# Scores as block-diagonal products and six product tiles in the head, in place of scores as 64-row tiles and four product tiles

## The chip, the cores and the metric

The kernel runs on one core of a Trainium2 chip. The metric is device time in microseconds, the median of three runs. The kernel before takes 285.92 us (285.66 to 286.01).

## The reference

Linear attention without a softmax, a root-mean-square norm for each head, then a two-layer network with an ELU between the layers, over 8 batches of 576 rows, 8 heads of 64:

```python
kv = np.einsum('bhsd,bhse->bhde', k, v)
out = np.einsum('bhsd,bhde->bhse', q, kv)
rms = np.sqrt(np.mean(out * out, axis=-1, keepdims=True) + 1e-06)
out = out / rms * g_norm
x = out.transpose(0, 2, 1, 3).reshape(B * S, H * D)      # 4608 x 512
h = x @ w_in                                             # 512 x 2048
g = np.where(h > 0.0, h, np.exp(np.minimum(h, 0.0)) - 1.0)
return g @ w_out                                         # 2048 x 512
```

Inputs and output are float32; the products run in bfloat16 with float32 sums.

## The kernel before, in words

The 4608 rows are cut into nine groups of 512. Group T from 0 to 7 holds the first 512 rows of batch T; group 8 holds the last 64 rows of all eight batches. Each group has an attention part and a network part. The network part is 128 TensorE products of 128x128 weights on 512 columns: 64 for the first layer (`mm1(T, i)`, i = 0 to 7, eight products each, two tiles of 512 columns of float32 in PSUM) and 64 for the second (`mm2(T, j, f0, f1)`, j = 0 to 3 blocks of 128 rows, sums over sixteen f; `mm2_quarter` does four f).

All instructions stand in an order written out by hand (`manual_schedule`). While group T runs its first layer and group T-1 its second, the attention of group T+1 is put between them: `kv` (72 tiles of 64x64), scores `se_mm`, squares, sums, `inv_rms` (Ln and Exp), `scale_rows`, then the turn to x transposed, by TensorE (`x_t`, groups 1 and 2) or by a DMA transpose (`x_dma`: pieces `xd`, then `xg` multiplies by g). `elu` follows each `mm1`: Exp on ScalarE, then on VectorE min(e, 1) - 1 and a max with h straight from PSUM; where `relu` is set, ScalarE also writes Relu(h) to SBUF (`elu_h`) and VectorE adds.

PSUM after the head: one `at` tile of two banks for attention, two `ps_m1` tiles of two banks, two `ps_m2` tiles of one bank. A tile's next user waits until the last has been read.

The scores (L202 to L220): for each of four row blocks j and four head pairs p, two 64-row products, one for each head l of the pair, on 64 columns of `kv_sb`, the two into different banks, so that two run beside each other. From group 3 on both halves of the scores are made after `mm1` step 3 (L760 to L762): half 0 in the `at` tile, half 1 in the two `ps_m2` tiles, from where ScalarE copies them to SBUF (`se_sb`, L283). `scale_rows` (L238) takes two VectorE steps for each half.

The head, group 0 (L482 to L671): all of it waits for loads. POOL issues them in order, k and v of batch 0 in eight pieces, w_in in four slices of 512 columns (L498), q of batch 1, then k and v of batch 1 around the first slice of w_out (L502 to L506); a ninth POOL load is issued only when the first has landed, and so on. Meanwhile TensorE turns q, makes kv and the scores of four column blocks c, transposed; squares go to ScalarE (`square_first`, A) but for the last, which VectorE makes in two steps (V: L585, L586); `mean_first` sums over a head by a product with a matrix of means; `log_first`, `exp_first` on ScalarE; `scale_first` on VectorE writes x0[c]. `idle` puts products with zeros between, into a bank that nobody reads. L663 to L671 then start the first layer with four product tiles (f = 0 to 3), c by c, and steps 2 to 7 follow, the turn of q of batch 1 in between (L680). L689 to L720 hold kv, scores and turns of batch 1 between the quarters of group 0's second layer; the w_out slices 1 to 3 are issued at L678 and L684.

Of the kernel before, what the change touches and what calls it, by code (L numbers as in the profile page):

```python
# [16 lines left out]
def kernel(  # L17
# [44 lines left out]
    kv_sb = const.tile([P, B, NPAIR, D], BF16, name="kv_sb")  # L62
# [72 lines left out]
    def load_w_in(s):  # L135
        cols = slice(s * 512, s * 512 + 512)
        nc.gpsimd.dma_start(  # L137
            out=w_in_sb[:, :, cols], in_=moe_w_in.rearrange("(c p) f -> p c f", p=P)[:, :, cols]
        )
# [13 lines left out]
    def q_tile(b):  # L153
        bf["q", b] = qkvp.tile([P, J, H, D], BF16, name="q_bf", tag="q")
        st = raw.pop(("q", b))
        if b < B:
            return st.rearrange("p (h j d) -> p j h d", h=H, j=J)
        return st.rearrange("p (j h d) -> p j h d", h=H, j=J)
# [26 lines left out]
    def q_t_single(q_pk, qt_ps, p):  # L185
        for j in range(J):
            for l in range(2):
                nc.tensor.transpose(
                    qt_ps[l * 64 : l * 64 + 64, p, j * P : j * P + P],
# [4 lines left out]
    def q_t_mm(q_sb, qt_ps, p):  # L194
        for j in range(J):
            nc.tensor.transpose(
                qt_ps[:, p, j * P : j * P + P],
                q_sb[:, j, 2 * p : 2 * p + 2, :],
                ident,
            )  # L200

    def se_mm(T, h, qT, banks):  # L202

        for jj in range(2):
            j = 2 * h + jj
            for p in range(NPAIR):
                s, u = p // 2, p % 2
                for t in range(1 if T < B else 2):
                    rows = slice(0, P) if T < B else slice(t * 64, t * 64 + 64)
                    for l in range(2):  # L210
                        ls = slice(l * 64, l * 64 + 64)
                        nc.tensor.matmul(  # L212
                            banks[l].rearrange("p (j u s e) -> p j u s e", j=2, u=2, s=2)[
                                rows, jj, u, s, :
                            ],
                            lhsT=qT(p, j)[ls, rows],
                            rhs=kv_sb[ls, T if T < B else 2 * j + t, p, :],
                            start=True,
                            stop=True,
                        )  # L220
# [17 lines left out]
    def scale_rows(xs, se, ss):  # L238
        for l in range(2):
            nc.vector.tensor_tensor(  # L240
                out=xs.rearrange("p j (u l s e) -> p l j u s e", u=2, l=2, s=2)[:, l].rearrange(
                    "p j u s e -> p (j u) s e"
                ),
                in0=se[:, l, :].rearrange("p (a s e) -> p a s e", s=2, e=D),
                in1=ss[:, 8 * l : 8 * l + 8]
                .rearrange("p (a s) -> p a s", s=2)
                .to_broadcast([P, 4, 2, D]),
                op=ALU.mult,
            )

    def attention(T):
        st = {}

        def q_t():
# [3 lines left out]
            for p in range(NPAIR):  # L258
                q_t_single(raw["q", T], qt_ps, p)
# [12 lines left out]
        def se(homes):  # L272

            for h, home in homes.items():
                if home is None:
                    home = at_tile(FP32).rearrange("p (l f) -> p l f", l=2)
                pair = isinstance(home, list)
                banks = home if pair else [home[:, l, :] for l in range(2)]
                se_mm(T, h, st["qT"], banks)
                if pair:  # L280
                    home = attp.tile([P, 2, G], FP32, name="se_sb", tag="se_sb", bufs=1)
                    for l in range(2):
                        nc.scalar.copy(home[:, l, :], banks[l])  # L283
                st["se", h] = home

        def norm(h):

            def squares():
                st["sq", h] = square(st["se", h], 2)
# [7 lines left out]
            def scale():  # L297
# [3 lines left out]
                scale_rows(rows, st.pop(("se", h)), st.pop(("ss", h)))  # L301

            return squares, sums, inv, scale
# [58 lines left out]
        def kv_out(us):  # L362
            nc.scalar.copy(
                kv_sb[:, T].rearrange("p (s u) e -> p s u e", s=2)[:, :, us],
                st["kv"][:, :, 0:P].rearrange("p s (u e) -> p s u e", u=2)[:, :, us],
            )
# [8 lines left out]
        pieces = {"kv": kv_all, "q": q_t, "qd": q_dma, "se": se}  # L375
# [6 lines left out]
        for h in range(2):  # L382
            for name, piece in zip(("sq", "sum", "inv", "mul"), norm(h)):
                pieces[f"{name}{h}"] = piece
# [5 lines left out]
    def mm1(T, i, cols=(slice(0, 512),), relu=False, spare=False, between=()):  # L390
# [4 lines left out]
        if spare:  # L395
            h_ps = [ps_m2.tile([P, G], FP32, name="h_ps", tag="mm2") for _ in range(2)]
            parts = [(a, a + 1, h_ps[a].rearrange("p (a t) -> p a t", a=1)) for a in range(2)]
        else:
            both = ps_m1.tile([P, 2, G], FP32, name="h_ps", tag="mm1")
# [91 lines left out]

    packed_kv(0)
# [5 lines left out]
    for s in range(4):  # L498
        load_w_in(s)
    fetch_packed_q(1)  # L500
    packed_kv(1)
    for name in "kv":  # L502
        fetch_packed_kv(name, 1, slice(0, 2))
    load_w_out(0)
    for name in "kv":
        fetch_packed_kv(name, 1, slice(2, 4))  # L506
# [9 lines left out]
    fetch_q(0)  # L516
# [17 lines left out]

# [331 lines left out]
```

## Time and profile before

| what | us |
|---|---|
| median of three runs | 285.92 |
| the profiled execution, its own time | 285.66 |
| its span, first to last instruction | 283.9 |
| TensorE busy | 274.1 |
| VectorE busy | 161.2 |
| ScalarE busy | 152.8 |
| POOL busy | 53.1 |
| from the first product of the first layer to the end of the span | 268.6 |

All times in the profile are counted from the start of the span; the profiled execution's own time holds 1.8 us more, around the span. The granted TensorE clock was 1.000. A timeline line has a start, a duration, engine and line, what is written and read, shapes and count, and in brackets the idle time before it with what ended it. A matmul's duration includes its way through the array, so the distance from one start to the next is what it costs on TensorE: 512 columns have a duration of 379 ns and a distance of 216 ns. Some matmul records are missing; the distance then still tells.

### The profile page before, as it was taken

What the parts mean: (1) busy time and instruction counts of PE and PEld (TensorE: products, weight loads), DVE (VectorE), ACT (ScalarE), POOL (GpSimd) and SP (SyncE); (2) the same over time, 40 slices, a digit from 0 to 9 for tenths busy, and PEclk for the clock granted to TensorE, in tenths of its full rate; (3) what the DMA queues carried; (4) which work ended last, traced back from release to release, by engine and by line L of the source; (5) the groups of instructions that cost most, each with busy time, mean ns of one, the idle gap of its engine ahead of it and who ended that gap; (6) DMA issues with size and microseconds to landing.
All of it is one profiled execution on the core that took longest, in us unless ns stands there. A gap on an engine that the chain in (4) does not pass through costs nothing.

```text
span 283.9 us, 5147 instructions
## 1 busy us (share of the span) xinstructions
PE 274.1 (97%) x2115; PEld 129.6 (46%) x2145; DVE 161.2 (57%) x235; ACT 152.8 (54%) x217; POOL 53.1 (19%) x93
## 2 busy tenths in 40 slices
PE   7899999999999999999999999999999999999994
PEld 2444454445444444444444444444444444444444
DVE  2458561779378646934694458544864486444400
ACT  2779544766496337633773378246923692333311
POOL 7834302341431241004210421002000000000000
PEclk9999999999999999999999999999999999999999
DMA  7999999797993596356953794355233123010122
GB/s 193 204 207 202 206 203 178 224 167 135 177 173 57 150 158 158 74 144 82 194 122 113 111 195 104 101 132 157 39 92 94 77 39 99 10 76 0 75 74 74
DMA packets 55963, 35.98 MB, mean 127 GB/s; under 512 B 32772, under 2 KB 53508, under 8 KB 55940
## 3 DMA queue, kind: packets, MB, share of 16 engines
q0 software_dynamic: 20192, 17.30, 39.7%
q1 hardware_dynamic: 35348, 17.83, 23.2%
q10 hardware_dynamic: 400, 0.52, 0.6%
q8 instruction: 16, 0.26, 0.4%
q14 instruction: 7, 0.06, 0.1%
HBM read 36.70 MB, written 9.44 MB: 163 GB/s over the span
## 4 chain that ended last, share of the span: by engine, by line
PE 80%; DMA 11%; DVE 4%; issue 1%; ACT 1%; POOL 1%; DVEq 0%; POOLq 0%
PE h_ps L406 36%; PE o_ps L453 36%; PE o_ps L825 5%; DMA w_in_sb<-in_moe_w_in_dram 5%; DMA w_out_sb<-in_moe_w_out_dram 5%; DMA k_pk<-in_k_dram 2%; PE at L177 1%; DVE gT L437 1%; DVE xs L240 1%; DVE ss L229 1%; POOL w_in_sb L137 1%; PE at L212 1%; PE se_ps L212 1%; DVE elu_e L429 0%; PE at L316 0%
## 5 line engine op out<-in xcount | busy, mean ns | idle before, releaser
L406 PE MATMUL h_ps<-xT,w_in_sb 128*128 128x512 bf16 x556 | 130.7, 379 | 0.3
L453 PE MATMUL o_ps<-w_out_sb,gT 128*128 128x512 bf16 x489 | 117.9, 379 | 1.8 <-DMA w_out_sb<-in_moe_w_out_dram 0.5
L418 ACT ACTIVATE elu_e<-h_ps 128x1024 bf16<-128x1024 f32 (+1 forms) x75 | 73.1, 982 | 82.6 <-PE h_ps L406 81.0
L406 PEld LDWEIGHTS <-w_in_sb 128*128 128x128 bf16 x560 | 53.2, 98 | 64.5 <-DVE xT L344 1.7
L453 PEld LDWEIGHTS <-gT 128*128 128x128 bf16 x512 | 49.8, 98 | 59.5 <-issue 0.3
L429 DVE TENSOR_SCALAR elu_e<-elu_e 128x1024 bf16<-128x1024 bf16 (+1 forms) x76 | 32.3, 425 | 75.4 <-ACT elu_e L418 75.4
L437 DVE TENSOR_TENSOR gT<-elu_e,h_ps 128x1024 bf16<-128x1024 bf16 (+1 forms) x56 | 64.1, 1145 | 5.8
L466 ACT COPY o_sb<-o_ps 128x512 f32<-128x512 f32 x32 | 18.5, 586 | 17.4 <-PE o_ps L453 17.4
L229 DVE TENSOR_REDUCE ss<-sq 128x16 f32<-128x1024 bf16 x16 | 19.3, 1217 | 7.7 <-ACT sq L224 6.9
L151 POOL COPY q_bf<-q_pk 128x512 bf16<-128x512 bf16 x24 | 14.9, 648 | 26.3 <-DMA q_pk<-in_q_dram 22.6
L424 ACT ACTIVATE elu_h<-h_ps 128x1024 bf16<-128x1024 f32 x19 | 19.3, 1015 | 0.0
L437 DVE TENSOR_TENSOR gT<-elu_e,elu_h 128x1024 bf16<-128x1024 bf16 x19 | 13.5, 713 | 3.6 <-ACT elu_h L424 2.4
L825 PE MATMUL o_ps<-w_out_sb,gT 128*128 128x512 bf16 (+1 forms) x79 | 14.0, 336 | 0.1
L125 POOL COPY gate<-qT 1x1 bf16<-1x1 bf16 x6 | 1.1, 179 | 61.5 <-DMA qT<-q_bf 61.5
L240 DVE TENSOR_TENSOR xs<-at,ss 128x512 bf16<-128x512 f32 x18 | 11.5, 681 | 1.2 <-ACT ss L236 1.2
L104 POOL DMA_DIRECT2D q_pk<-in_q_dram x14 | 10.6, 764 | 3.6 <-issue 1.9
L825 PEld LDWEIGHTS <-gT 128*128 128x128 bf16 x80 | 7.7, 98 | 6.4 <-DVE gT L437 0.4
L224 ACT ACTIVATE sq<-at 128x1024 bf16<-128x1024 f32 x9 | 9.4, 1044 | 1.5 <-PE at L212 1.5
L118 POOL DMA_DIRECT2D k_pk<-in_k_dram x12 | 8.4, 700 | 5.4 <-DMA w_in_sb<-in_moe_w_in_dram 2.5
L118 POOL DMA_DIRECT2D v_pk<-in_v_dram x12 | 8.5, 708 | 2.2 <-DMA w_in_sb<-in_moe_w_in_dram 1.8
L833 ACT COPY o_last<-o_ps 128x512 f32<-128x512 f32 (+1 forms) x5 | 2.5, 500 | 10.8 <-PE o_ps L825 10.8
L177 PEld LDWEIGHTS <-k_pk 64*64 64x64 bf16 x576 | 6.5, 107 | 3.8 <-issue 3.6
(71 smaller groups left out, 123.0 us busy)
## 6 DMA issues: line engine op xcount, KB each, us to landing
out_dram<-o_sb SPq DMA_DIRECT2D x16, 512.0 KB, 3.0
q_pk<-in_q_dram POOLq DMA_DIRECT2D x14, 256.0 KB, 5.3
k_pk<-in_k_dram POOLq DMA_DIRECT2D x6, 576.0 KB, 8.4
v_pk<-in_v_dram POOLq DMA_DIRECT2D x6, 576.0 KB, 11.5
w_in_sb<-in_moe_w_in_dram POOLq DMA_DIRECT2D x4, 512.0 KB, 10.6
w_out_sb<-in_moe_w_out_dram POOLq DMA_DIRECT2D x4, 512.0 KB, 15.3
st_q<-in_q_dram SPq DMA_DIRECT2D x2, 512.0 KB, 4.8
st_q<-in_q_dram SPq DMA_DIRECT2D x16, 64.0 KB, 2.5
```

The lines of the kernel that those rows point to most:

```text
L118: nc.gpsimd.dma_start(out=raw[name, b].rearrange("p h j d -> p h (j d)")[:, hs], in_=in_[:, hs])
L151: eng.tensor_copy(out=out_, in_=in_)
L229: nc.vector.reduce_sum(out=ss, in_=sq.rearrange("p c (h e) -> p (c h) e", h=H), axis=AX.X)
L240: nc.vector.tensor_tensor(out=xs.rearrange("p j (u l s e) -> p l j u s e", u=2, l=2, s=2)[:, l].rearrange("p j u s e -> p (j u) s e"), in0 ...
L406: nc.tensor.matmul(h_ps[a][:, cs], lhsT=w_in_sb[:, c, f * P : f * P + P], rhs=x(c, cs), start=(c == 0), stop=(c == KC - 1),)
L418: nc.scalar.activation(e[:, lo:hi, :], ps, AF.Exp)
L424: nc.scalar.activation(h[:, lo:hi, :], ps, AF.Relu)
L429: nc.vector.tensor_scalar(out=e[:, lo:hi, :], in0=e[:, lo:hi, :], scalar1=1.0, scalar2=1.0, op0=ALU.min, op1=ALU.subtract,)
L437: nc.vector.tensor_tensor(out=gT[T][:, 2 * i + lo : 2 * i + hi, :], in0=e[:, lo:hi, :], in1=h, op=ALU.add if relu else ALU.max,)
L453: nc.tensor.matmul(o_ps[T, j], lhsT=gT[T][:, f, j * P : j * P + P], rhs=w_out_sb[:, f, :], start=(f == 0), stop=(f == FC - 1),)
L466: nc.scalar.copy(o_sb[T][:, j % 2, :], o_ps.pop((T, j)))
L825: nc.tensor.matmul(ps, lhsT=gT[B][:, f, j * P : j * P + P], rhs=w_out_sb[:, f, cols], start=(f == 0), stop=(f == FC - 1),)
```

## The change

Scores: `bd_kv` replaces `kv_sb`. It holds for each pair of heads a 128x128 matrix with the two heads' kv on the diagonal and zeros beside them (a memset once). One product of 128 rows on 128 columns replaces the two 64-row tiles; in the last group two products with 64 weight columns replace four tiles. `kv_out` writes the two diagonal blocks in two ScalarE copies. `scale_rows` becomes one VectorE step. From group 3 on, half 0 of the scores is made after `mm1` step 1 and half 1 after step 3, both in the `at` tile, with sums and scale one step later each, and no product takes the Relu path; the second layer's pieces stand at steps 0 to 6. In group 1 half 0 of the scores of batch 2 moves into the first layer (after step 6), and its two turns stand together.

Head: the six products of steps 0 to 2 start in the head's own banks, w_in comes in five slices, the w_out slices 0 and 1 are issued ahead of k and v of batch 1, the fourth square goes to ScalarE, blocks 0 to 2 take other places among the idle products, and the mean of block 3 follows the first four products. q of batch 0 is cast into a tile in the order of the head pairs. Steps 3 to 7 follow; then the second layer's quarter 0, the turn of q of batch 1, three pieces of quarter 1, kv of batch 1, the last piece, and its scores.

```diff
-    kv_sb = const.tile([P, B, NPAIR, D], BF16, name="kv_sb")
+    bd_kv = const.tile([P, B, NPAIR, P], BF16, name="bd_kv")
...
-    def se_mm(T, h, qT, banks):
-
-        for jj in range(2):
-            j = 2 * h + jj
-            for p in range(NPAIR):
-                s, u = p // 2, p % 2
-                for t in range(1 if T < B else 2):
-                    rows = slice(0, P) if T < B else slice(t * 64, t * 64 + 64)
-                    for l in range(2):
-                        ls = slice(l * 64, l * 64 + 64)
-                        nc.tensor.matmul(
-                            banks[l].rearrange("p (j u s e) -> p j u s e", j=2, u=2, s=2)[
-                                rows, jj, u, s, :
-                            ],
-                            lhsT=qT(p, j)[ls, rows],
-                            rhs=kv_sb[ls, T if T < B else 2 * j + t, p, :],
-                            start=True,
-                            stop=True,
-                        )
+    def se_mm(T, j, qT, se_ps):
+
+        ov = se_ps.rearrange("p (u l s e) -> p u l s e", u=2, l=2, s=2)
+        for p in range(NPAIR):
+            s, u = p // 2, p % 2
+            if T < B:
+                nc.tensor.matmul(
+                    ov[:, u, :, s, :],
+                    lhsT=qT(p, j),
+                    rhs=bd_kv[:, T, p, :],
+                    start=True,
+                    stop=True,
+                )
+            else:
+                for l in range(2):
+                    nc.tensor.matmul(
+                        ov[l * 64 : l * 64 + 64, u, :, s, :],
+                        lhsT=qT(p, j)[:, l * 64 : l * 64 + 64],
+                        rhs=bd_kv[:, 2 * j + l, p, :],
+                        start=True,
+                        stop=True,
+                    )
...
+    def scale_rows(xs, se_ps, ss, n):
+        nc.vector.tensor_tensor(
+            out=xs.rearrange("p c (h e) -> p (c h) e", h=H),
+            in0=se_ps.rearrange("p c (h e) -> p (c h) e", h=H),
+            in1=ss.to_broadcast([P, n * H, D]),
+            op=ALU.mult,
+        )
...
+        def se(h):
+
+
+            def product(se_ps=None):
+                if se_ps is None:
+                    se_ps = at_tile(FP32).rearrange("p (c f) -> p c f", c=2)
+                for c in range(2):
+                    se_mm(T, 2 * h + c, st["qT"], se_ps[:, c, :])
+                st["se", h] = se_ps
+                st["sq", h] = square(se_ps, 2)
...
+            bd_v = bd_kv[:, T].rearrange("p (s u) e -> p s u e", s=2)
+            for l in range(2):
+                ls = slice(l * 64, l * 64 + 64)
+                nc.scalar.copy(
+                    bd_v[ls, :, us, ls],
+                    st["kv"][ls, :, 0:P].rearrange("p s (u e) -> p s u e", u=2)[:, :, us],
+                )
...
+    edges = (0, 512, 768, 1280, 1664, 2048)
+    for lo, hi in zip(edges, edges[1:]):
+        load_w_in(slice(lo, hi))
+    load_w_out(0)
     fetch_packed_q(1)
+    load_w_out(1)
     packed_kv(1)
-    for name in "kv":
-        fetch_packed_kv(name, 1, slice(0, 2))
-    load_w_out(0)
-    for name in "kv":
-        fetch_packed_kv(name, 1, slice(2, 4))
+    for hs in (slice(0, 2), slice(2, 4)):
+        for name in "kv":
+            fetch_packed_kv(name, 1, hs)
...
+    nc.vector.memset(bd_kv, 0.0)
...
-    def square_first(c, eng):
-        if eng is A:
-            nc.scalar.activation(sq0[c], se0[c], AF.Square)
-        else:
-            nc.vector.tensor_copy(out=r0[c], in_=se0[c])
-            nc.vector.tensor_tensor(out=sq0[c], in0=r0[c], in1=se0[c], op=ALU.mult)
+    def square_first(c):
+        nc.scalar.activation(sq0[c], se0[c], AF.Square)
...
+    def first(fs, cs):
+        for c in cs:
+            for f in fs:
+                nc.tensor.matmul(
+                    products[f],
+                    lhsT=w_in_sb[:, c, f * P : f * P + P],
+                    rhs=x0[:, c, :],
+                    start=(c == 0),
+                    stop=(c == KC - 1),
+                )
+
+    qt_ps = turned(7)
+    turn_first(qt_ps, (2,))
+    nc.scalar.copy(qT0[:, 2, :], qt_ps[:, 0, :])
     kv_first(0)
+    idle(idle_ps, 1)
+    se0[0] = bank(6)
+    se_first(0)
+    square_first(0)
+    qt_ps = turned(0)
+    turn_first(qt_ps, (3,))
+    nc.vector.tensor_copy(out=qT0[:, 3, :], in_=qt_ps[:, 0, :])
+    idle_ps = bank(3)
+    kv_first(1)
+    mean0[0] = bank(2)
+    mean_first(0)
+    log_first(0)
+    se0[1] = bank(7)
+    se_first(1)
+    square_first(1)
+    exp_first(0)
+    g_ps = bank(1)
     nc.tensor.matmul(
         g_ps[:, 0:1],
         lhsT=g_row.rearrange("p l d -> p (l d)"),
...
         stop=True,
     )
     nc.vector.tensor_copy(out=g_col, in_=g_ps[:, 0:1])
     kv_first(2)
+    idle(idle_ps, 2)
+    se0[2] = bank(1)
+    se_first(2)
+    square_first(2)
+    mean0[1] = bank(0)
     mean_first(1)
     log_first(1)
     exp_first(1)
+    idle(idle_ps, 1)
     kv_first(3)
+    scale_first(0)
     idle(idle_ps, 1)
+    mean0[2] = bank(2)
     mean_first(2)
     log_first(2)
+    se0[3] = bank(3)
+    se_first(3)
+    square_first(3)
     exp_first(2)
+    idle(bank(0), 6)
     scale_first(1)
     scale_first(2)
+    pair = ps_head.tile([P, 2, G], FP32, name="h_ps", tag="kv")
+    products = {0: pair[:, 0, :], 1: pair[:, 1, :], 2: bank(6), 3: bank(7), 4: bank(0)}
+    first((0, 1, 2, 3), (0,))
+    mean0[3] = bank(2)
     mean_first(3)
     log_first(3)
     exp_first(3)
     scale_first(3)
+    first((0, 1, 2, 3), (1,))
+    first((4,), (0, 1))
+    first((0, 1, 2, 3, 4), (2,))
+    products[5] = bank(1)
+    first((5,), (0, 1, 2))
+    first((0, 1, 2, 3, 4, 5), (3,))
+    gT[0] = mlpg.tile([P, FC, G], BF16, name="gT", tag="gT")
+    single = [
+        [(a, a + 1, products[2 * i + a].rearrange("p (a t) -> p a t", a=1)) for a in range(2)]
+        for i in (1, 2)
+    ]
+    for i, parts in enumerate([[(0, 2, pair)]] + single):
+        elu(0, i, parts, i == 1)()
...
+    for i in range(3, 8):
+        mm1(0, i, relu=i in (3, 5, 7), home={5: "m2", 6: "at"}.get(i, "m1"))()
+    for l in range(2):
+        ls = slice(l * 64, l * 64 + 64)
+        nc.gpsimd.tensor_copy(
+            out=bd_kv[ls, 0].rearrange("p (s u) e -> p u s e", s=2)[:, :, :, ls], in_=kv0[ls]
+        )
+    for s in (2, 3):
+        load_w_out(s)
     fetch_packed_q(2)
     packed_kv(2)
     for name in "kv":
         fetch_packed_kv(name, 2)
     both = ps_m1.tile([P, 2, G], FP32, name="o_ps", tag="mm1")
     for a in range(2):
         o_ps[0, 2 + a] = both[:, a, :]
     order = (2, 3, 0, 1)
     for j in order:
         mm2_quarter(0, j, 0)
+    at["q"]()
+    for j in order[:3]:
+        mm2_quarter(0, j, 1)
+    at["kv0"]()
     at["kv1"]()
+    mm2_quarter(0, order[3], 1)
+    at["se0"]()
+    at["se1"](ps_m1.tile([P, 2, G], FP32, name="se_ps", tag="mm1"))
     for n in range(2):
         at[f"sum{n}"]()
         at[f"inv{n}"]()
     at["mul0"]()
     at["mul1"]()
     for j in order:
         mm2_quarter(0, j, 2)
     unpack_q(2, Q)
     ahead["qd"]()
     for j in order:
         mm2(0, j, 12, FC, hold=j in (2, 3))
+        if j == 2:
+            at["x0"]()
+        if j == 0:
+            at["x1"]()
...
+    def group(T, at, start, second, relu=()):
+
+
+        early, late = {}, {}
+        for name, i in start.items():
+            if name in ("se0", "se1"):
+                early.setdefault(i + 1, []).extend(("sum" + name[2], "inv" + name[2]))
+                late.setdefault(i + 1, []).insert(0, "mul" + name[2])
+            late.setdefault(i, []).append(name)
+        for i in range(9 if 8 in early else 8):
+            if i == 8:
+                for name in early[8] + late[8]:
+                    at[name]()
+                break
+            rest = mm1(
+                T, i, (slice(0, 512),), i in relu, between=[at[name] for name in early.get(i, ())]
+            )
             for piece in second.get(i, ()):
+                mm2(*piece)
+            names = late.get(i, [])
+            if i in relu and names[:1] in (["mul0"], ["mul1"]):
+                at[names.pop(0)]()
             rest()
+            for name in names:
+                at[name]()
...
+        if i == 6:
+            at["se0"]()
...
+        second = {i: [(T - 1, i // 2, 8 * (i % 2), 8 * (i % 2) + 8)] for i in range(8)}
+        if T > 2:
+            mm2(*second[0][0])
+            second = {i - 1: second[i] for i in range(1, 8)}
+        else:
+            quarters = [(1, 2 + i // 4, 4 * (i % 4), 4 * (i % 4) + 4) for i in range(2, 8)]
+            second = {i + 1: [piece] for i, piece in enumerate(quarters)}
+        at, start = ahead, {}
+        if T + 1 < NT:
+            start = {"kv": 0, "se0": 1, "xd0": 2, "se1": 3, "xd1": 4, "xg0": 5, "xg1": 6}
         if T + 2 < NT:
             at["landed"]()
             fetch(T + 2)
             ahead = attention(T + 2)
+        group(T, at, start, second, (1, 2, 4) if T == 2 else ())
```

## The prediction

> **What bounds the kernel now.** I read the busy shares and the chain of waits first, then TensorE's time by group, then its order of instructions in the groups and in the head.
>
> ```profile
> PE 274.1 (97%) x2115; PEld 129.6 (46%) x2145; DVE 161.2 (57%) x235; ACT 152.8 (54%) x217; POOL 53.1 (19%) x93
> PE 80%; DMA 11%; DVE 4%; issue 1%; ACT 1%; POOL 1%; DVEq 0%; POOLq 0%
> ```
> TensorE is busy nearly always, but busy is not the same as useful. So I cut the span where each group's first product starts.
>
> ```profile
> 0.00:15.34 15.34, 11.88 (x120) 5.51 (x122) 6.36 (x19) 8.35 (x13) 11.62 (x23) 1.00 0.99 200
> 15.34:47.69 32.35, 31.17 (x277) 15.51 (x280) 18.73 (x30) 20.64 (x31) 9.12 (x14) 1.00 1.27 205
> 47.69:72.67 24.98, 24.77 (x224) 11.99 (x224) 17.92 (x27) 15.87 (x24) 6.97 (x14) 1.00 0.85 179
> 72.67:93.63 20.96, 20.56 (x190) 9.62 (x193) 14.83 (x21) 13.79 (x19) 5.92 (x9) 1.00 0.74 118
> 93.63:122.76 29.13, 28.97 (x231) 13.56 (x233) 18.35 (x26) 16.54 (x23) 5.59 (x10) 1.00 0.67 127
> 210.17:238.56 28.39, 28.23 (x190) 12.95 (x192) 17.48 (x24) 15.73 (x22) 0.00 (x0) 1.00 0.28 75
> 238.56:266.21 27.65, 27.54 (x127) 12.43 (x128) 13.15 (x16) 10.09 (x12) 0.00 (x0) 1.00 0.10 40
> ```
> The columns are the stretch, its length, then busy time and count of PE, PEld, DVE, ACT, POOL. The last row is the last group's, with no attention beside it: 128 products of 512 columns in 27.65, 0.216 us each, without a gap. Groups 3 to 6 take 29.13 (29.14): the same 128, and 1.48 for the next group's attention. There is no other idle time there, so what an edit puts on TensorE or takes off it in these groups is the change of the time.
>
> ```profile
> 69.90 0.61 PE L316 MATMUL at<-ident,xs 128*128 128x128 bf16 x8
> 70.35 1.03 PE L453 MATMUL o_ps<-w_out_sb,gT 128*128 128x512 bf16 x4
> 106.53 1.89 PE L406 MATMUL h_ps<-xT,w_in_sb 128*128 128x512 bf16 x8
> 108.35 0.41 PE L212 MATMUL at<-kv_sb,qT 64*128 64x64 bf16 x16
> 108.59 0.40 PE L212 MATMUL se_ps<-kv_sb,qT 64*128 64x64 bf16 x16
> 108.92 1.90 PE L406 MATMUL h_ps<-xT,w_in_sb 128*128 128x512 bf16 x8
> 25.80 1.08 PE L188 MATMUL at<-ident,q_pk 128*64 128x128 bf16 x32
> 26.81 0.39 PE L406 MATMUL h_ps<-xT,w_in_sb 128*128 128x512 bf16 x1
> 36.44 5.34 PE L453 MATMUL o_ps<-w_out_sb,gT 128*128 128x512 bf16 x23 [0.37 <-DMA w_out_sb<-in_moe_w_out_dram]
> ```
> First column start, second duration; the distance of starts is what an instruction costs.
>
> **Scores, groups 3 to 6.** Removed: 32 tiles of 64 rows. The 8 products from 106.53 would let the next start at 108.26; it starts at 108.92, so the scores cost 0.66, 0.09 of it a gap ahead of the first. Added: 16 products of 128x128 over 128 columns (block-diagonal bd_kv). This product is not in the trace; the nearest row is the turn L316, the same shape in and out: 8 in 0.45 and no gap ahead or behind, 0.90 for 16. Bounds for one: 32 ns, the pitch of the half-wide L188 (32 in 1.01), would give 0.51; 82 ns (4 turns and a change of tile shape, 7.47 to 7.80) 1.31. I take 0.90, as the shape is the same: +0.24 four times, **+0.96** (-0.6 to +2.6).
>
> The Trainium skill, TensorE: Matmul & The Clock Gate, section Back-to-back issue gap, speaks against the change: pairs of weight load and product of 128 columns sustain about 81 ns. The row above shows 56 ns; by the page the four groups would lose about 2.6 in place of 0.96. I go by the row.
>
> **Scores elsewhere.** Group 7 (for the last, mixed rows): 64 tiles now, 222.27 to 224.74 less 8 products, 0.74. Then 32 products with 64 weight columns, L188's form: 1.01, and a 0.09 change of shape in each half: 1.19, **+0.45**. Groups 1 and 2: 0.89 and 2 x 0.44 now against 0.90: **+0.03**.
>
> **The head.** The chain to product 1 runs through squares, mean, Ln, Exp and scale of four column blocks. I walk it with today's durations (square 0.60, Ln 0.69, Exp 0.63, on ScalarE 0.11 less from start to start; scale 0.75; product 0.216, result after 0.38).
>
> ```profile
> 13.65 0.69 DVE L585 COPY r<-bank 128x512 f32<-128x512 f32 x1 [0.50 <-PE bank L573]
> 14.37 0.69 DVE L586 TENSOR_TENSOR sq<-r,bank 128x512 bf16<-128x512 f32 x1
> 15.12 0.39 PE L589 MATMUL bank<-sq,means 128*128 128x512 bf16 x1
> 15.34 0.38 PE L665 MATMUL at<-xT,w_in_sb 128*128 128x512 bf16 x1
> 16.93 0.75 DVE L598 SCALAR_TENSOR_TENSOR xT<-bank,g_col,r 128x512 bf16<-128x512 f32 x1 [0.54 <-ACT r L595]
> 17.93 0.59 PE L665 MATMUL h_ps<-xT,w_in_sb 128*128 128x512 bf16 x2
> ```
> Now the fourth square is two VectorE steps that end at 15.06; the mean waits for them, and the first product behind it starts at 15.34. Twelve products cover the way of block 3 from that mean to the end of its scale, 17.68.
>
> After: scores 0 at 8.6 (8.84 now), 1 at 10.1, 2 at 11.7, block 3 at 13.35; scale 0 ends 13.95, scale 1 14.85. The fourth square, on ScalarE behind Ln 1, Exp 1 and Ln 2, ends 15.1, no sooner. But the mean of block 3 stands behind four products, and six idle products end at 14.90, so product 1 starts at **14.90, -0.44** (14.7 to 15.34). Block 3's mean is then at 15.77 and its scale ends 18.35, 0.67 late; the 18 products ahead of its use end at 19.0, so that is covered by 0.65. With twelve it would cost 0.65. All 24 end at 20.30.
>
> **Group 0, rest.** Banks 4 and 5 (pair) go to product step 4, which could start at 22.03. Its holder's Exp starts 19.64, then min and max on VectorE (0.5 and 1.22 from start to start), free at 22.44: a new stall of 0.46. The first product ends at 29.39; now 30.37 with the turn of q (1.11) in it. From there: quarter 0 (3.45), turn (1.11), 12 products, so the two k/v products at 36.73; now they wait for ScalarE (0.38) and then TensorE for w_out slice 1 (0.37). These waits go, as slice 1 is loaded ahead of k and v. What is late next is k and v: the same bytes stand ahead of their second half as ahead of slice 1 now, so it lands about 36.4, used at 37.26, 0.85 of cover. Slices 2 and 3 keep their place (last landing 25.83 + 16.2 = 42.0, used at 43.17). The copies for bd_kv on POOL ahead of them (one of 0.54 now, two then) hide behind a queue that issues some 15 us before landing. Scores at 38.81, scaled by 44.1 and 45.2; the turns wait 0.09, the second's eviction (VectorE, 0.75) has 4 products (0.86) over it and costs 0.14. Group 1 starts at **47.76 against 47.69, +0.07**. Bounds: w_out slice 3 at 42.06, 16 products, two turns and 0.25 give 46.7 (-1.0); no gain in the head and these stalls twice, 48.5 (+0.8).
>
> **Covered.** memset of bd_kv: 0.27 for 256 words today, so about 1.8 for 2048, in VectorE's wait for q (1.7 to 4.75); without it 1.8 on the head. w_in in five: slice 0 lands 7.2 after its issue at 7.31, 14.5, and the next, half as wide, about 1.5 later; it is used at 16.9. Second ScalarE copy of kv (0.37), less 2 x 0.59 of score copies and 2 x 1.02 of Relu a group: off the path. In return VectorE reads two more products from PSUM (1.22 in place of 0.71) and scales in one step (as 1.22, now 1.29): 17.5 becomes about 18.4 of 29.4. Scores move to product 1: qT lands by 128.5 where POOL's gate read it; they would start near 132.3, 3.8 of cover. The last piece of the second product moves from step 7 to 6: the same 16 products. Group 1: the stall ahead of 72.67 (0.15) goes, the earlier turn waits about as long: -0.03. Group 2: its 0.26 wait near 91.7 hangs on VectorE, which saves 0.14: **-0.1**.
>
> **Sum.** 0.96 + 0.45 + 0.03 + 0.07 - 0.13 = +1.38. The profiled execution took 285.66 (span 283.9 and 1.8 around it); that gives 287.04. The median of the three, 285.92, lies 0.26 above it; I name **287.1**.
>
> **Rivals.** (A) Not slower: group 0 gets all that the loads allow. With no stall behind 14.90 it ends by landing, 46.7: -1.0 in place of +0.07, sum +0.31, 285.9 to 286.2. For it: 0.75 of waits that go. Against: the hold of the pair, from durations alone. It decides from group 1 at 47.1 or earlier, and only a further 0.6 would be faster. (B) VectorE becomes the bound in groups 3 to 7: the scores of half 1 need the at bank that half 0's scale frees, 1.1 ahead by my walk; late by 1.4, five groups lose 0.3: 288.5. For: 1.0 more PSUM reading a group. Against: group 2 runs this order in shorter steps and loses 0.26. (C) The new order of loads only moves the wait: k and v land at 38.2 rather than 36.4 and hold TensorE 0.9: 287.9. For: cover of 0.85 only. Against: equal bytes. (D) The scores run at the upper bound, 82 ns: 2.6, 0.7 and 0.9 in place of 0.96, 0.45 and 0.03: 289.8; L316 is against it.
>
> **Chances.** Forecast 0.55 (its own range 286.5 to 287.7), A 0.23, B 0.1, C 0.09, D 0.03. Within 0.2% (285.35 to 286.49, about what the measurement can tell) comes from A and the forecast's low edge: 0.2; faster, A's far end: 0.1; slower 0.7. The range leaves out D, B's far half and A's far end: 286.0 to 288.1.
>
> **What would show it.** First product at 14.9; step 4 of group 0 held by VectorE near 22; no wait for w_out slice 1, TensorE not waiting for k_pk; group 1 at 47.8; 8 scores in 0.45 with no gap; groups 3 to 6 29.36 long, group 7 28.84. I am wrong if group 1 starts before 47.1, or groups 3 to 6 stay at 29.13, or VectorE ends waits of TensorE there.

## The result, and the profile after

The changed kernel takes 287.98 us (median of six runs, 287.60 to 288.20), the kernel before 285.87 (285.66 to 287.35) beside it: a ratio of 1.0065, 95% interval 1.0043 to 1.0086. By the medians it is slower by about 2.1 us. The profiled execution took 288.11 us with a span of 285.8, against 285.66 and 283.9.

First the busy shares and the chain of waits of the changed kernel, then TensorE alone in the same stretches as before: each begins with the first product of a group of rows (the columns are the stretch, its length, busy time of PE and its instructions, then clock, DMA share and GB/s).

```profile
PE 277.1 (97%) x1976; PEld 133.8 (47%) x2006; DVE 166.6 (58%) x216; ACT 144.5 (51%) x209; POOL 54.4 (19%) x95
...
PE 93%; DMA 2%; DVE 2%; ACT 1%; issue 1%; SPq 0%; DVEq 0%
```

```profile
0.00:15.14 15.14, 12.66 (x124) 1.00 1.02 201
15.14:48.25 33.11, 31.74 (x261) 1.00 1.28 205
48.25:73.30 25.05, 24.94 (x207) 1.00 0.81 170
73.30:94.10 20.80, 20.64 (x175) 1.00 0.77 120
94.10:123.43 29.33, 29.17 (x214) 1.00 0.73 130
182.10:211.54 29.44, 29.28 (x214) 1.00 0.44 108
211.54:240.52 28.98, 28.82 (x159) 1.00 0.28 73
240.52:268.14 27.62, 27.46 (x126) 1.00 0.10 39
```

Loads have nearly left the chain of waits (11% before, 2% now), and TensorE stands in 93% of it. That looks better and is not: what TensorE has to do became longer. Set against the old stretches, the loss lies here:

| place | before | after | difference |
|---|---|---|---|
| group 1 starts (head and group 0) | 47.69 | 48.25 | +0.56 |
| group 1 | 24.98 | 25.05 | +0.07 |
| group 2 | 20.96 | 20.80 | -0.16 |
| groups 3 to 6 together | 116.54 | 117.44 | +0.90 |
| group 7 | 28.39 | 28.98 | +0.59 |
| group 8 | 27.65 | 27.62 | -0.03 |

The sum is +1.93, the whole of the span's growth. The rest of the profiled execution's +2.45 lies around the span: 1.8 us in the profiled execution of before, 1.9 to 2.3 in the six of the changed kernel. No run explains it.

The next rows are the changed kernel's order of time in the head and in group 0 (start, duration, engine, line, operation; the bracket is the idle time ahead of the row and what ended it).

```profile
13.84 1.47 PE L521 MATMUL bank<-zeros 128*128 128x512 bf16 x6
15.14 0.59 PE L599 MATMUL h_ps<-xT,w_in_sb 128*128 128x512 bf16 x2
...
21.46 1.22 DVE L422 TENSOR_TENSOR gT<-elu_e,h_ps 128x1024 bf16<-128x1024 bf16 x1
22.74 3.61 PE L391 MATMUL h_ps<-xT,w_in_sb 128*128 128x512 bf16 x16 [0.31 <-DVE gT L422]
...
36.90 0.48 PE L174 MATMUL at<-v_pk,k_pk 64*64 64x64 bf16 x36
38.02 0.48 PE L174 MATMUL at<-v_pk,k_pk 64*64 64x64 bf16 x36 [0.65 <-ACT bd_kv L345]
39.31 0.61 PE L197 MATMUL at<-bd_kv,qT 128*128 128x128 bf16 x8
39.75 0.61 PE L197 MATMUL se_ps<-bd_kv,qT 128*128 128x128 bf16 x8
40.20 4.48 PE L438 MATMUL o_ps<-w_out_sb,gT 128*128 128x512 bf16 x20
...
48.25 1.02 PE L391 MATMUL h_ps<-xT,w_in_sb 128*128 128x512 bf16 x4
```

Two waits stand out. Step 4 of the first layer starts at 22.74, just behind VectorE's maximum on the pair (21.46 and 1.22). And the second k/v product stands still 0.65 behind ScalarE's copies of the first into bd_kv. The wait for a w_out slice, which stood here before, is gone. Each run of eight score products takes 0.44 or 0.45 from start to start, and no gap follows it.

One trace stands behind each of these starts, and the start of the head varies: four kernels with this same head have their first product at 15.14, 15.16, 15.30 and 15.14 (changed, e1_tiled, e2_kvgap, e3_relu0). So a difference below 0.2 in the start of group 1 can come from the head alone; distances that begin behind it don't hold this.

### The profile page after: what moved, and what is told of

Its sections match the earlier page's. It is cut to its first block, busy times and chain, and to the rows that moved or that the text cites. A ratio compares the mean times of both kernels' runs of the same rounds, so it can differ in the third digit from the quotient of the medians.

```text
span 285.8 us, 4842 instructions
## 1 busy us (share of the span) xinstructions
PE 277.1 (97%) x1976; PEld 133.8 (47%) x2006; DVE 166.6 (58%) x216; ACT 144.5 (51%) x209; POOL 54.4 (19%) x95
## 4 chain that ended last, share of the span: by engine, by line
PE 93%; DMA 2%; DVE 2%; ACT 1%; issue 1%; SPq 0%; DVEq 0%
PE h_ps L391 41%; PE o_ps L438 37%; PE o_ps L819 5%; DMA st_q<-in_q_dram 2%; PE at L197 2%; PE at L174 2%; PE bank L599 1%; PE bank L521 1%; ACT elu_e L403 1%; PE h_ps L599 1%; PE at L391 1%; PE bank L569 1%; PE at L295 0%; DVE gT L422 0%; PE kv_ps L174 0%
## 5 line engine op out<-in xcount | busy, mean ns | idle before, releaser
L391 PE MATMUL h_ps<-xT,w_in_sb 128*128 128x512 bf16 x540 | 127.4, 379 | 0.6 <-DVE gT L422 0.3
L403 ACT ACTIVATE elu_e<-h_ps 128x1024 bf16<-128x1024 f32 (+1 forms) x72 | 70.9, 994 | 82.2 <-PE h_ps L391 80.1
L422 DVE TENSOR_TENSOR gT<-elu_e,h_ps 128x1024 bf16<-128x1024 bf16 (+1 forms) x63 | 74.8, 1187 | 6.6
L216 ACT ACTIVATE sq<-at 128x1024 bf16<-128x1024 f32 x14 | 14.3, 1023 | 12.6 <-PE at L197 10.1
L231 DVE TENSOR_TENSOR xs<-at,ss 128x1024 bf16<-128x1024 f32 x14 | 17.0, 1218 | 1.2 <-ACT ss L228 1.2
L521 PE MATMUL bank<-zeros 128*128 128x512 bf16 x23 | 7.7, 463 | 1.4 <-DVE zeros L497 1.2
L197 PEld LDWEIGHTS <-qT 128*128 128x128 bf16 x112 | 7.3, 98 | 3.1
L409 ACT ACTIVATE elu_h<-h_ps 128x1024 bf16<-128x1024 f32 (+1 forms) x9 | 8.4, 965 | 0.0
```

The costliest lines, as they stand in the source:

```text
L216: nc.scalar.activation(sq, se_ps, AF.Square)
L231: nc.vector.tensor_tensor(out=xs.rearrange("p c (h e) -> p (c h) e", h=H), in0=se_ps.rearrange("p c (h e) -> p (c h) e", h=H), in1=ss.to_b ...
L391: nc.tensor.matmul(h_ps[a][:, cs], lhsT=w_in_sb[:, c, f * P : f * P + P], rhs=x(c, cs), start=(c == 0), stop=(c == KC - 1),)
L403: nc.scalar.activation(e[:, lo:hi, :], ps, AF.Exp)
L422: nc.vector.tensor_tensor(out=gT[T][:, 2 * i + lo : 2 * i + hi, :], in0=e[:, lo:hi, :], in1=h, op=ALU.add if relu else ALU.max,)
```

## The experiments

### Which edit costs the groups with attention: e1_tiled and b1_diag

The change does two things to the scores: another form (block-diagonal products in place of 64-row tiles) and another place (half 0 and half 1 at two steps in place of one). e1_tiled is the changed kernel with the old form; it still reads k/v from bd_kv, so ScalarE's two copies stay. b1_diag is the old kernel with the new form. Here and below only the lines of an edit that matter are shown.

```diff
 e1_tiled, against the changed kernel
-                    lhsT=qT(p, j),
-                    rhs=bd_kv[:, T, p, :],
+                            lhsT=qT(p, j)[ls, rows],
+                            rhs=bd_kv[ls, T if T < B else 2 * j + t, p, ls],
 b1_diag, against the kernel before
-                se_mm(T, h, st["qT"], banks)
+                for c in range(2):
+                    se_mm(T, 2 * h + c, st["qT"], banks[c])
```

> The changed kernel with the scores of groups 1 to 8 as 64-row tiles again (two heads into two banks, scaling in two VectorE steps); order, Relu choice, loads and group 0 as in the changed kernel. Theory (the scores' cost on TensorE is what groups 3 to 7 lose): groups 3 to 6 go from 29.33 to 29.15 to 29.3 each (16 scores at a time in 0.34 and 0.10 of change of tile shape against 0.45, twice, so 0 to 0.2 each), group 7 from 28.98 to about 28.5, the time falls by 0.5 to 1.3 us. Rival B (VectorE and the missing Relu path cost it): groups 3 to 6 stay at 29.33 or grow by the extra VectorE step, the time stays within 0.3 us.

> The kernel before, with only its scores in the form of the changed kernel: 8 products of 128 columns for each half, on the block-diagonal k/v, in the old place (both halves together) and with everything else in the old order. Theory 'a group pays by how many runs of scores it has and in which form' (both halves together in 64-row tiles: 0.57 and a change of shape of 0.09, 0.66; 8 products of 128 columns: 0.45 wherever they stand): groups 3 to 6 take 29.13 + 0.90 - 0.66 = 29.37 (29.33 to 29.40) each, group 7 has 32 products with 64 weight columns in one run, about 1.05 + 0.09 in place of 0.74, 28.75 to 28.85, group 2's window stays near 20.9, group 1 still starts near 47.7; sum +0.96 + 0.4: 287.1 to 287.5. Rival 'only the split costs, the form is free': groups 3 to 6 stay at 29.13 and the time stays within 0.5 of 285.9.

e1_tiled took 287.82 us, ratio 1.0058 (1.0035 to 1.0081). Groups 3 to 6 stayed at 29.33 three times and 29.44; group 7 fell by 0.40 to 28.58. The theory, 29.15 to 29.3 and a gain of 0.5 to 1.3 us, missed in groups 3 to 6 and in the time; 29.33 is what its rival B (VectorE) had named. b1_diag took 287.39, ratio 1.0059 (1.0037 to 1.0081): groups 3 to 6 took 29.35 each, group 7 28.77, both where the first theory had put them; the span is 285.4. These are rows of the order of time: first e1_tiled, then b1_diag.

```profile
131.22 1.89 PE L438 MATMUL o_ps<-w_out_sb,gT 128*128 128x512 bf16 x8
133.05 0.41 PE L200 MATMUL at<-bd_kv,qT 64*128 64x64 bf16 x16
133.39 1.47 PE L391 MATMUL h_ps<-xT,w_in_sb 128*128 128x512 bf16 x6
```

```profile
108.53 0.61 PE L208 MATMUL at<-bd_kv,qT 128*128 128x128 bf16 x8
108.97 0.61 PE L208 MATMUL se_ps<-bd_kv,qT 128*128 128x128 bf16 x8
109.42 1.89 PE L408 MATMUL h_ps<-xT,w_in_sb 128*128 128x512 bf16 x8
...
225.22 0.64 PE L217 MATMUL at<-bd_kv,qT 128*64 128x128 bf16 x16
225.69 0.61 PE L217 MATMUL se_ps<-bd_kv,qT 128*64 128x128 bf16 x16
226.24 1.90 PE L408 MATMUL h_ps<-xT,w_in_sb 128*128 128x512 bf16 x8
```

Read the distances of starts. In e1_tiled eight products of 512 columns begin at 131.22; at 0.216 each the tiles could start at 132.95 and start at 133.05, and the next product starts 0.34 later: 0.44 for a half, as much as eight products of 128 columns (0.44 to 0.45). In b1_diag both halves cost 0.89. Four kernels make the full square (groups 3 to 6, then group 7):

| | both halves at one step | a half at each of two steps |
|---|---|---|
| 64-row tiles | before: 29.13, 28.39 | e1_tiled: 29.33, 28.58 |
| block-diagonal | b1_diag: 29.35, 28.77 | changed: 29.33, 28.98 |

So a run of tiles costs by itself: 32 tiles in one run take 0.57 and 0.09 ahead of them, 16 take 0.34 and 0.10. The difference, 0.22, is the work of 16 tiles; the other 0.2 of each run doesn't grow with the tiles and comes with the change of shape and back, as runs in the full shape have none of it. What in the change takes the time, no run shows. Split in two, the tiles pay it twice and lose all that they gain. The full-width products pay none, so they cost 0.9 wherever they stand. The right column also has the second layer's pieces in other places and no Relu path, but these add nothing: 27.62 for the products (group 8), 0.80 for k/v with its change of shape and 0.89 for the scores make 29.31 of the 29.33, and in these groups the traces of e1_tiled and of the changed kernel list no wait of TensorE for VectorE. So rival B, whose number came, has the wrong cause.

In group 7 the new products have 64 weight columns and pay it as well: 1.02 and 0.09 in one run (b1_diag), twice 0.57 and 0.09 in two. In groups 3 to 6 either edit alone, form or split, costs 0.2, and the second adds nothing; in group 7 the split costs 0.19, the form 0.38 and both 0.59. The rival for b1_diag, that the form is free, is out. In groups 3 to 6 e1_tiled gave nothing back; reasoning from the form alone holds for group 7 only.

The Trainium skill states a cause that fits in TensorEngine Tiling (Array Packing), section Key Properties: a change of tiling mode drains TensorE. No run here shows the drain itself, and the page gives no price; these runs give about 0.2 us for a run in another shape, there and back.

### What holds group 0: e2_kvgap, e3_relu0, e4_idle3

Each mends one wait of the changed kernel.

```diff
 e2_kvgap
-    for j in order[:3]:
+    for j in order[:2]:
         mm2_quarter(0, j, 1)
     at["kv0"]()
+    mm2_quarter(0, order[2], 1)
     at["kv1"]()
 e3_relu0
-        elu(0, i, parts, i == 1)()
+        elu(0, i, parts, i == 0)()
 e4_idle3
-    idle(bank(0), 6)
+    idle(bank(0), 3)
```

> The changed kernel with one piece of the second product (four products) moved between the two k/v products of batch 1 in group 0. Theory (the second k/v product waits 0.65 us for ScalarE's copies of the first out of the same PSUM tile): that wait goes, group 1 starts 0.5 to 0.7 us sooner than 48.25. Rival C (the loads of k and v of batch 1 are late): the wait stays, group 1 within 0.15 us of 48.25.

> The changed kernel with the Relu path in step 0 of group 0 in place of step 1, so that ScalarE frees the pair's banks. Theory (step 4 waits 0.47 us for VectorE's max on step 0): the wait goes, steps 4 to 7 come 0.3 to 0.5 us sooner, and group 1 with them, as no load is reached before 48.25 less 0.5. Rival (the loads or the chain of group 1's attention set the end of group 0): steps come sooner, group 1 stays within 0.15 us of 48.25.

> The changed kernel with three idle products in place of six ahead of the first layer of group 0. Theory (idle products set the start at 15.14, the scales of blocks 0 and 1 end at 14.1 and 14.8 and the first w_in slice lands at 14.3): the first product starts near 14.5, 0.6 us sooner, and group 1 0.4 to 0.65 us sooner. Rival (the chain through the mean of block 3 sets the end of the 24 products): the start moves, the 24 products still end near 20.5 and group 1 stays.

**e2_kvgap** took 287.66, ratio 1.0056 (1.0039 to 1.0073). Its order of time:

```profile
36.44 0.48 PE L174 MATMUL at<-v_pk,k_pk 64*64 64x64 bf16 x36 [0.19 <-ACT qT L248]
36.85 1.04 PE L438 MATMUL o_ps<-w_out_sb,gT 128*128 128x512 bf16 x4
37.82 0.48 PE L174 MATMUL at<-v_pk,k_pk 64*64 64x64 bf16 x36
38.23 1.04 PE L438 MATMUL o_ps<-w_out_sb,gT 128*128 128x512 bf16 x4
```

The four products between the two halves cover ScalarE's copies: both halves take 0.41 and the 0.65 is gone. Group 1 starts at 48.05, 0.20 earlier, where the theory had 0.5 to 0.7. The first half now waits 0.19 for ScalarE's copy of qT, which the old order had covered, and the second half pays a change of shape of its own (it starts at 37.82, where the four products from 36.85 would let it start at 37.71). The head of this trace is also 0.16 late: from the first product to group 1 it takes 32.75 in place of 33.11, so 0.36 of the 0.65 is gained.

**e3_relu0** was a miss: 288.49, ratio 1.0083 (1.0056 to 1.0109), with group 1 at 49.00. The intervals overlap, but its six spans, 286.0 to 286.7, all lie above the changed kernel's, 285.7 to 285.9: it is slower.

```profile
20.53 5.44 PE L391 MATMUL h_ps<-xT,w_in_sb 128*128 128x512 bf16 x24
26.94 1.89 PE L391 MATMUL at<-xT,w_in_sb 128*128 128x512 bf16 x8 [0.97 <-DVE gT L422]
```

With the Relu moved to step 0, ScalarE frees the pair early, and step 4 no longer waits: 24 products run in one stretch from 20.53. But step 6 lies in the head's bank of step 2, and its holder is freed by VectorE. VectorE now has four single maxima (0.69) with four small minima (0.29, one of them 0.66) in a row for steps 1 and 2, so the bank comes free near 26.9. A wait of 0.31 became one of 0.97.

**e4_idle3** took 287.52, ratio 1.0051 (1.0035 to 1.0067). The first product starts at 14.56 in place of 15.14, and group 1 at 48.02 in place of 48.25:

```profile
14.56 0.61 PE L599 MATMUL h_ps<-xT,w_in_sb 128*128 128x512 bf16 x2
15.00 0.59 PE L599 MATMUL bank<-xT,w_in_sb 128*128 128x512 bf16 x2
15.43 0.38 PE L581 MATMUL bank<-sq,means 128*128 128x512 bf16 x1
15.65 0.59 PE L599 MATMUL h_ps<-xT,w_in_sb 128*128 128x512 bf16 x2
16.08 1.31 PE L599 MATMUL bank<-xT,w_in_sb 128*128 128x512 bf16 x4
16.78 3.14 PEld L599 LDWEIGHTS <-w_in_sb 128*128 128x128 bf16 x16 [0.61 <-DMA w_in_sb<-in_moe_w_in_dram]
17.23 0.59 PE L599 MATMUL h_ps<-xT,w_in_sb 128*128 128x512 bf16 x2
...
20.25 1.03 PE L391 MATMUL h_ps<-xT,w_in_sb 128*128 128x512 bf16 x4
```

Of the 0.58 gained at the first product 0.29 is left behind the 24 products (20.25 against 20.54): the 20 behind the mean take 4.60 in place of 4.32. All of it is lost at one place: the four products from 16.08 take 1.15 to the next start, where four cost 0.86. The last two of them (f = 4) are the first that use the second slice of w_in, and their weight load waited 0.61 for that slice, until 16.78. So a load gives the gain back, and not the chain of block 3 that the rival named: block 3's scale ends at 17.98 and is first used at 18.96. The start of group 1, 0.23 sooner, lies between what theory and rival had.

The times of e2_kvgap and e4_idle3 can't be told from the changed kernel's (their intervals overlap with its); the traces show which wait went and where the rest stayed.

### Group 0 alone: b2_group0 and b3_best

b2_group0 is the old kernel with the changed head and group 0, in old scores and old order from group 1 on. b3_best adds the edits of e2_kvgap and e4_idle3 to it.

```diff
 b2_group0: the changed head and group 0, with
-    at["se0"]()
-    at["se1"](ps_m1.tile([P, 2, G], FP32, name="se_ps", tag="mm1"))
+    at["se"]({0: None, 1: ps_m1.tile([P, 2, G], FP32, name="se_ps", tag="mm1")})
+    for n in range(2):
+        at[f"sq{n}"]()
 b3_best, against b2_group0
-    for j in order[:3]:
+    for j in order[:2]:
         mm2_quarter(0, j, 1)
     at["kv0"]()
+    mm2_quarter(0, order[2], 1)
     at["kv1"]()
...
-    idle(bank(0), 6)
+    idle(bank(0), 3)
```

> The kernel before with the changed head and the changed group 0 alone (six product tiles in the head's banks, loads in the new order, w_in in five slices, half of the second product ahead of group 1's attention); scores stay 64-row tiles with both halves together, and groups 1 to 8 run in the old order. Theory 'group 0 itself costs half a microsecond by two waits (VectorE's maximum, the second k/v product behind ScalarE's copy)': group 1 starts at 48.2 (48.0 to 48.3) in place of 47.69, groups 3 to 6 at 29.13, group 7 at 28.39; 286.2 to 286.6. Rival 'group 1 starts late because the scores ahead of it are untiled': group 1 at 47.7 to 47.9 and 285.9 to 286.1.

> As b2_group0, with the two mends of group 0 tried before together: a quarter of the second product between the two halves of the k/v product, and 3 idle products in place of 6 ahead of the first layer. Theory 'each wait mended alone gave 0.2': group 1 at 47.75 to 47.9, old groups behind it, 285.9 to 286.2, no better than before. Rival 'the waits add up to what group 0 loses, and more': group 1 at 47.3 to 47.6 and 285.5 to 285.8, faster than both kernels. Other rival 'the next wait takes each over': group 1 at 48.0 and 286.2 to 286.4.

b2_group0 took 286.03 against 285.71 beside it, ratio 1.0005 (0.9992 to 1.0017), span 284.2, group 1 at 47.85, groups 3 to 6 at 29.13 and group 7 at 28.39. The time and the start of group 1 fall into the rival's ranges: 0.16 of the 0.56 comes with the order of group 0, no more than the head varies, and 0.40 with the new form of the scores and of their k/v (the first product at 15.14 in place of 15.04 is within what the head varies). But the rival's reason is wrong; it isn't the score products. e1_tiled, which has the old products on the new bd_kv, starts group 1 at 48.23. From the first k/v product to group 1 it takes 11.32, the changed kernel 11.35 and b2_group0 11.05: 0.27 comes with bd_kv and 0.03 with the products. Rows of ScalarE and TensorE, first the changed kernel's copies (its wait of 0.65 is shown above), then b2_group0:

```profile
37.44 0.53 ACT L345 CAST bd_kv<-at 64x128 bf16<-64x128 f32 x2 [1.20 <-PE at L174]
```

```profile
37.34 0.27 ACT L352 CAST kv_sb<-at 128x128 bf16<-128x128 f32 x1 [1.20 <-PE at L174]
37.66 0.48 PE L174 MATMUL at<-v_pk,k_pk 64*64 64x64 bf16 x36 [0.38 <-ACT kv_sb L352]
```

The block-diagonal form needs the same k/v as two copies of 64 rows; each takes as long as one copy of 128 rows, and the second half of the k/v product waits for both: 0.65 idle against 0.38. The two halves write different columns of the one tile, so nothing that is being read is overwritten; whether a tile for each half would take the wait away was not tried. b1_diag shows the two copies in the old order, where the scores follow the second half and wait for them. First the kernel before, then b1_diag:

```profile
35.43 0.41 PE L212 MATMUL at<-kv_sb,qT 64*128 64x64 bf16 x16 [0.38 <-ACT kv_sb L363]
```

```profile
35.75 0.61 PE L208 MATMUL at<-bd_kv,qT 128*128 128x128 bf16 x8 [0.65 <-ACT bd_kv L365]
```

The scores cost 0.58 in b2_group0 and 0.89 in the changed kernel, but most of that is covered: from the start of the scores to group 1 they take 8.82 and 8.94, as in b2_group0 the first turn behind them starts 0.21 behind the products ahead of it, just after VectorE's scale.

b3_best took 285.76, ratio 0.9996 (0.9983 to 1.0009), group 1 at 47.47: the two mends add up (-0.38 against b2_group0) and bring group 1 0.22 ahead of the kernel before. Those are the numbers of the rival; the gain that it named can't be told from none.

### What is left in its first layer: f1_relu1257 and f3_relu0257

e3_relu0 showed which two banks VectorE holds. If ScalarE frees both, the wait should go and not move.

```diff
 f1_relu1257, against b3_best
-        elu(0, i, parts, i == 1)()
+        elu(0, i, parts, i in (1, 2))()
...
-        mm1(0, i, relu=i in (3, 5, 7), home={5: "m2", 6: "at"}.get(i, "m1"))()
+        mm1(0, i, relu=i in (5, 7), home={5: "m2", 6: "at"}.get(i, "m1"))()
 f3_relu0257: the same with (0, 2) in the first
```

> b3_best with the steps of group 0 that take the way through ScalarE's Relu changed from 1, 3, 5, 7 to 1, 2, 5, 7. ScalarE's work stays the same; on VectorE step 2's two pieces of 0.29 + 0.69 become 0.42 + 0.69, and step 3's 0.42 + 0.69 becomes 0.42 + 1.22. Theory 'the first layer of group 0 waits for VectorE alone': step 4 still stands 0.31 behind the maximum on the pair (it reads it until 22.3), so little is gained: group 1 at 47.4 to 47.5, 285.6 to 285.8. Rival 'ScalarE is as late': a new wait of 0.2 to 0.5 ahead of steps 5 to 7, group 1 at 47.7 to 48.0, 286.0 to 286.3.

> b3_best with Relu steps 0, 2, 5, 7 in group 0. With Relu in step 0 ScalarE frees the pair near 21.5, before step 4 wants it at 22.0, and with Relu in step 2 the bank under step 6's tile is freed by ScalarE near 24.8 (where Relu in step 0 alone left it to VectorE until 26.9, in e3_relu0). Theory 'the first layer waits for VectorE's maxima on the head's banks': steps 3 to 7 lose their 0.31 + 0.1, the first layer ends 0.3 to 0.45 earlier than in b3_best (28.8 to 28.95), group 1 at 47.0 to 47.2, 285.3 to 285.6, the first to beat the kernel before, by about 0.1%. Rival 'another engine or load takes the wait over' (step 1's maxima now on VectorE, or w_in's last slice): the first layer ends at 29.25 or later, group 1 at 47.4 to 47.9, 285.7 to 286.3.

f1_relu1257 took 285.49 against 285.77, ratio 0.9988 (0.9979 to 0.9997); f3_relu0257 285.37, ratio 0.9983 (0.9974 to 0.9992). What TensorE waited for between 19 and 49 us (engine, line, what it waited for, total, times, longest), first b3_best, then f3_relu0257, and f3_relu0257's first layer:

```profile
PE at L174 <- ACT qT L250: 0.4, 1, 0.4
PE h_ps L398 <- DVE gT L429: 0.3, 1, 0.3
```

```profile
PE at L174 <- ACT qT L250: 0.4, 1, 0.4
PE o_ps L445 <- issue: 0.2, 1, 0.2
```

```profile
20.20 5.34 PE L398 MATMUL h_ps<-xT,w_in_sb 128*128 128x512 bf16 x24
25.38 1.89 PE L398 MATMUL at<-xT,w_in_sb 128*128 128x512 bf16 x8
27.28 1.89 PE L398 MATMUL h_ps<-xT,w_in_sb 128*128 128x512 bf16 x8
29.00 3.62 PE L445 MATMUL o_ps<-w_out_sb,gT 128*128 128x512 bf16 x15
```

The wait ahead of step 4 is gone. A shorter one takes its place ahead of step 7: the eight products from 25.38 would let it start at 27.11, and it starts at 27.28, just behind a maximum of VectorE (26.00 and 1.22); a product's duration hides it from the lists. The lists also begin behind a wait of 0.23 for the second slice of w_in, at 16.74. Steps 3 to 7 take 8.80 in place of 9.10, the layer ends at 29.00 and group 1 starts at 47.22, just past the 28.8 to 28.95 and 47.0 to 47.2 expected. This is the best version: by a sixth of a per cent faster than the kernel before, the new group 0 with the old scores behind it. f1_relu1257 kept the 9.10 and starts group 1 at 47.54, near its theory's 47.4 to 47.5; its time is below what either theory gave it and can't be told from that of f3_relu0257. So what the freed wait is worth, 0.3 in the first layer, is shown by the traces and not by the times. The eleven spans of f3_relu0257, 283.5 to 283.8, and the twelve of b3_best, 283.7 to 284.1, agree with it.

## Why the prediction was right, and where its steps were off

The side was right, and the time lies in the range: 287.1 named (286.0 to 288.1), 287.98 measured, and 287.04 worked out against 288.11 of the profiled execution. It lies there by 0.12 only. The forecast's own range, 286.5 to 287.7, ends below it; the stated range is wider as it takes in rival C and the near half of B, and the time lies beside C's 287.9 without C's cause. That it fell inside is in part luck. Term by term:

- **Scores, groups 3 to 6: right, with a reason that lacked a half.** +0.96 predicted, +0.90 measured: 0.20 in each group (29.33 for 29.36), and 0.11 in group 6 that lies in its k/v product and not in the scores. The row L316 gave 0.45 for eight, and eight took 0.45. The price was put on the form alone, by comparing with 32 tiles in one run. The split that comes in the same change would have cost the tiles the same 0.2 a group, as e1_tiled shows. The sum was right; to keep the tiles and split them, as one could have concluded from it, would have gained nothing. The bounds of 32 and 82 ns were both far from the 56 ns found. On the rule that the prediction weighed: the runs never showed 81 ns; the same page, TensorE: Matmul & The Clock Gate, has 55.6 ns for a warm array in its section "Wait — 56ns, not 53.3ns?", and that is what the trace has.
- **Group 7: mis-sized by 0.14.** +0.45 predicted, +0.59 measured. The step took 1.01 for 32 products in one run and added 0.09 in each half; a run of 16 takes 0.57, not 0.51, as each run has its tail.
- **The head: mis-sized by 0.24.** First product at 14.90 predicted, 15.14 measured. The six idle products began at 13.84, 0.24 later than the walk; their length (1.30) and the order behind them were right. Some of the 0.24 may be the head's own variation (15.14 to 15.30). The second slice of w_in, which the walk had land at about 16.0, held e4_idle3 until 16.78. The fourth square ended at 15.04 (14.45 and 0.59; predicted 15.1).
- **Step 4 held by VectorE near 22: right** in place and size. Step 3's 8 products run from 20.54 and would let it start at 22.27; it starts at 22.74, 0.47 late, predicted 0.46. f3_relu0257 shows the mechanism by taking it away, and e3_relu0 that the next bank is close behind.
- **The k/v products: this step failed.** The prediction wrote that the second ScalarE copy of k/v (0.37) is "off the path". That holds from group 1 on, where the copies follow the whole k/v run of 72 products and nothing waits for them. In group 0 the second half is written to the tile that the copies of the first are reading, and TensorE waited 0.65 for two copies of 64 rows. The walk had k/v and the four products behind it at 2.08 from start to start (36.73 to 38.81); they took 2.41: the first half 1.12 where the walk had 0.53, the second with the four products 1.29 where it had 1.55. With 0.17 left of the late head that makes group 1 start 0.49 later than the predicted 47.76. e2_kvgap took this wait away, b2_group0 cut it to 0.38 by a single copy, and in b1_diag the two copies hold the scores as long.
- **No wait for w_out slice 1, none for k_pk: right.** The order of time shows neither.
- **Groups 1 and 2:** -0.10 predicted (0.03 for scores, -0.13 for waits), -0.09 measured. A wait of 0.21 behind the second half of the scores in group 1 stayed (0.23 before); the walk had counted it as gone.
- **Rivals.** (A) Group 1 at 47.1 or earlier: it started at 48.25. (B) VectorE the bound in groups 3 to 7: 27.62 for the products, 0.80 for k/v with its change of shape and 0.89 for scores make 29.31 of the 29.33, so nothing waits there. (C) Late k and v: the halves started at 36.90 with no wait for a load. (D) 82 ns: 56 measured.

The terms add to +1.93 against +1.38, and 0.49 of the 0.55 is group 0.

## What to carry to other kernels

Price a run of small tiles between full-width products as a fixed cost for the change of shape plus the tiles, and compare forms only in the number of runs that the new order will have: moving the work may cost what its form saves. When a product is split so that its second half goes to the tile from which another engine copies the first, the copy is on the path of both; put other products between the halves. When a held bank stalls a step, look at who frees the next bank before the work is moved: one held bank freed earlier made e3_relu0 slower, two let the first layer of f3_relu0257 end 0.25 sooner than b3_best's.

## What the runs showed of the hardware

- A run of TensorE work in another tile shape carries about 0.2 us that doesn't grow with its length: 64-row tiles 0.66 for 32 and 0.44 for 16 with the gap ahead; products of 64 weight columns 1.11 for 32 and 0.66 for 16. Tiles of 64x64 were run in four lengths, 0.47 for 32 (e1_tiled, group 7), 0.52 for 36 (e2_kvgap), 0.74 for 64 (before, group 7) and 0.80 for 72 (k/v): about 0.008 for each and 0.2 for the run. Products of 128 by 128 between products of 512 columns carry nothing: 0.45 for 8, 0.89 for 16.
- Two ScalarE copies of 64 rows took 0.53, one of 128 rows 0.27: half the rows did not make a copy shorter.
- A dense group repeats to 0.01 us within one execution (29.33, 29.33, 29.34), where six times of the whole kernel spread by 0.6. So an edit of 0.2 in one stage is read from its stage, and only the sum from the times. Group 6 takes 29.44 in the changed kernel and in e1_tiled, 0.11 of it in its k/v product (0.82 in place of 0.71); why was not followed.
